# An attention and two-MoE-layer kernel in fp32 on one core: GpSimd's arithmetic given to VectorE and ScalarE, with shorter start-up groups and a new instruction list

## The chip, the cores and the metric

The kernel runs on one core of a Trainium2 chip. The metric is the device time of one execution in microseconds (us). Three runs of the kernel before took 591.71, 591.72 and 592.02 us; the median, 591.72, is the time before. A core has five engines that are spoken of here: TensorE (PE), VectorE (DVE), ScalarE (ACT), GpSimd (POOL) and SyncE (SP), which issues the transfers.

## What is computed

A sparse attention is followed by two feed-forward layers, all in float32 with inputs of 2 batches, 8 heads, 768 positions and head size 64, that is 1536 tokens of width 512.

```python
k_sum = k.reshape(B, H, nb, 32, D).max(axis=3)
v_sum = v.reshape(B, H, nb, 32, D).mean(axis=3)
scores_l = scale * q @ k.T                     # kept where |i - j| < 16
scores_s = scale * q @ k_sum.T + log(32)
a = softmax(concat([scores_l, scores_s]))
x = a @ concat([v, v_sum])
...
xn = x / sqrt(mean(x * x) + 1e-6) * rms_g
x = (silu(xn @ w_gate) * (xn @ w_val)) @ w_out     # d_ff 1536
...
h = x @ w_in
out = where(h > 0, h, exp(min(h, 0)) - 1) @ w_out2   # d_ff 2048
```

## The kernel before

**Attention.** Each batch is worked off in 6 pairs of 64-position tiles, so there are 12 pairs. For a tile the program builds `ka` (`copy_keys`: 96 neighbouring keys and the 24 block maxima `ksum`), the scores of a pair's two head halves come out of PE (`scores`, L462), DVE adds the mask and takes the row maximum (`add_mask` L467, `row_max` L471; the first four pairs get their mask from PE in `premask`), ACT does the exponentials and their sums (`exps`, L478), `guard` (L484) adds 1e-9 to the sums, `invert` (L488) takes reciprocals, `normalize` (L493 to L498) multiplies, PE transposes (`turn_e`, L503, tile `at`), a copy makes `ats`, PE applies the values `va` (`apply_v2`, L515, tile `pv`), and a copy puts the result into `xT`. The block means of `v` are placed into one of four `va` tiles (`place_v`) and repeated into the others (`repeat_v`, L375).

**Feed-forward.** The 1536 tokens are three blocks of 512. fp32 products are made of three fp32r products of high and low parts, so each operand is split: a cast makes the high part (L135, on ACT) and a subtraction the low part (L146, tiles `ws` for weights, `act..l` for activations). Weights come as 64-bit floats (`st`) and are turned into fp32 (`raw`) in `convert_a`, `convert_l`, `convert_b` (L259 to L279): DVE does that in two passes (L270, L279), or ACT and DVE in one each (L267, L275). Block 0 goes through both layers by itself, one chunk of 128 hidden columns at a time (`pg`, `pv_..c`, tanh gate `th` in L727 to L738, then `acc`; in the second layer `ph`, `ex`, `acc`), beside the attention of the later tokens. Blocks 1 and 2 are then done jointly with seven half-size products in place of eight (`add_joint`, L937 and L1116, tiles `w_1u`, `wd`, `td`). Norms go through sums of squares (`square`, `add_square` L589), a power on POOL (`root`, L607) and a diagonal product on PE.

**What sets the order.** Every operation is added with the engines it may run on, a cost and a due time (`add`, a dictionary of engines and costs where there is a choice), but the order of issue is a list of numbers written into the file, `PLAN`: each number divided by 4 names the operation, the remainder which of its engines takes it. `TAGS` says which of the PSUM banks or buffers a tile gets where it has a choice. The list was made ahead from the costs. Each engine executes its instructions in the list's order, so an instruction that waits holds up all behind it on that engine.

**POOL's part before.** Besides masks, selectors, zeros and the roots, POOL has 6 normalisations, 2 copies of keys, 4 repeats of `va`, 2 additions of squares, 24 low parts of weights (8 `ws_g`, 5 `ws_v`, 4 `ws_o`, 2 `ws_i`, 5 `ws_p`) and 5 of activations. The choices come from these lines:

```python
ANY_2 = {DVE: 0.6}, {POOL: 1.28, DVE: 0.6}, {POOL: 1.28}
...
LO_0, LO_1 = (1, 1, 1), 0
```

`LO_0` picks the entry of `ANY_2` for the weights of block 0.

**The start.** While the first keys are on their way PE multiplies zeros (`keep_warm`, L1227, tile `warm`) in groups, each `WARM_LONG.get(i, 2)` products long; a group in `AFTER_K` first multiplies a piece of a loaded key tile, so it can't begin ahead of that load. Group 1, behind the tile kT_0, has eight.

## Time and profile before

| | |
|---|---|
| median of three runs | 591.72 us |
| profiled execution: own time | 592.67 us |
| profiled execution: span from the first to the last instruction | 591.0 us |
| busy: PE, DVE, ACT, POOL | 574.1, 547.3, 430.4, 69.6 us |
| mean TensorE clock granted | 1.00 of full speed |
| bytes moved by transfers | 108.79 MB, 184 GB/s |

All rows quoted below are of that one profiled execution, whose own time is 0.95 us over the median. Busy times are unions of instructions' spans; instructions of one engine overlap a little in the trace, so the spacing from start to start is the price of one in a row. "Idle before" names the instruction that ended the engine's wait. A chain of waits is followed back from the last instruction of the stretch asked for, at each step to what released it.

### The profile page before, as it was taken

How to read it: one execution, taken by the hardware profiler on the slowest of the kernel's cores; microseconds unless marked ns; L12 is line 12 of the kernel's file. 1: busy time of each engine (PE TensorE's matmuls, PEld its weight loads, DVE VectorE, ACT ScalarE, POOL GpSimd, SP SyncE). 2: the span in 40 equal slices, each digit the busy share in tenths (PEclk: the TensorE clock that was granted, in tenths of full speed). 3: DMA queues.
4: the chain of work that ended last, by engine and by line, in shares of the span. 5: the costliest groups of instructions: out<-in, count | busy, mean ns of one | idle time of the engine just before them, and what ended most of it. 6: DMA issues, size and time to landing. Idle time of an engine off the chain costs nothing.

```text
span 591.0 us, 9948 instructions
## 1 busy us (share of the span) xinstructions
PE 574.1 (97%) x3366; PEld 467.6 (79%) x3366; DVE 547.3 (93%) x1049; ACT 430.4 (73%) x953; POOL 69.6 (12%) x89
## 2 busy tenths in 40 slices
PE   7799989999999999999999999999999999999997
PEld 3588768788877888888888888888888888888886
DVE  5999999999989988989998999999999999999993
ACT  3889978998988988646534456676666989788750
POOL 3326425024100031100000000000000000000000
PEclk9999999999999999999999999999999999999999
DMA  8888889988978977142134416324316552742202
GB/s 318 287 297 280 303 303 321 325 300 282 312 231 273 318 232 265 55 159 71 55 91 161 143 50 188 92 81 142 107 38 196 200 159 78 244 129 65 71 35 107
DMA packets 56051, 108.79 MB, mean 184 GB/s; under 512 B 6784, under 2 KB 19584, under 8 KB 56000
## 3 DMA queue, kind: packets, MB, share of 16 engines
q1 hardware_dynamic: 56000, 108.16, 56.2%
q8 instruction: 26, 0.43, 0.3%
q14 instruction: 25, 0.20, 0.1%
HBM read 79.82 MB, written 28.31 MB: 183 GB/s over the span
## 4 chain that ended last, share of the span: by engine, by line
PE 81%; DVE 9%; ACT 6%; issue 2%; DMA 1%; POOL 0%; DVEq 0%; ACTq 0%; POOLq 0%
PE acc L766 11%; PE B_1u L937 8%; PE ph L710 7%; PE C_1u L937 6%; PE A_1u L937 6%; PE B_2d L1116 6%; PE B_2u L937 6%; PE B_1d L1116 4%; PE C_2d L1116 4%; PE A_2d L1116 4%; PE C_2u L937 4%; PE A_2u L937 4%; PE C_1d L1116 3%; PE A_1d L1116 3%; PE pg L710 2%
## 5 line engine op out<-in xcount | busy, mean ns | idle before, releaser
L710 PE MATMUL ph<-xa,ws_i 128*128 128x512 f32 x192 | 48.0, 395 | 0.6 <-DVE ex L747 0.6
L937 PE MATMUL B_1u<-xh,w_1u 128*128 128x512 f32 x144 | 47.8, 391 | 0.0
L710 PEld LDWEIGHTS ph<-xa,ws_i 128*128 128x128 f32 x192 | 35.5, 188 | 8.8 <-DVE ex L747 1.0
L710 PE MATMUL pg<-xs,ws_g 128*128 128x512 f32 (+1 forms) x168 | 36.4, 364 | 0.7 <-DVE th L734 0.7
L1116 PE MATMUL B_2d<-td,wd 128*128 128x512 f32 x144 | 34.6, 389 | 0.0
L146 DVE TENSOR_TENSOR wd<-rd,wd 128x512 fp32r<-128x512 f32 x49 | 32.8, 684 | 0.2 <-ACT wd L135 0.2
L937 PE MATMUL C_1u<-xh,w_1u 128*128 128x512 f32 x96 | 32.8, 390 | 0.0
L710 PEld LDWEIGHTS pg<-xs,ws_g 128*128 128x128 f32 x168 | 28.1, 189 | 5.5 <-DVE th L734 0.9
L937 PE MATMUL A_1u<-xh,w_1u 128*128 128x512 f32 x96 | 32.3, 390 | 0.0
L135 ACT CAST wd<-rd 128x512 fp32r<-128x512 f32 x49 | 29.1, 621 | 4.1 <-PE B_2u L937 2.2
L937 PEld LDWEIGHTS B_1u<-xh,w_1u 128*128 128x128 f32 x144 | 27.0, 188 | 6.1 <-ACT h_1u L135 0.3
L937 PE MATMUL B_2u<-xh,w_2u 128*128 128x512 f32 x96 | 31.6, 389 | 0.0
L1116 PEld LDWEIGHTS B_2d<-td,wd 128*128 128x128 f32 x144 | 27.0, 188 | 5.6
L937 PE MATMUL B_1u<-xl,w_1u 128*128 128x512 f32 x72 | 28.1, 390 | 0.0
L1116 PE MATMUL B_1d<-td,wd 128*128 128x512 f32 x108 | 26.5, 389 | 0.0
L478 ACT ACTIVATE e<-e,nm 128x120 f32<-128x120 f32 x64 | 24.5, 387 | 1.7 <-DVE nm L471 1.6
L135 ACT CAST td<-z 128x512 fp32r<-128x512 f32 x28 | 17.1, 619 | 11.7 <-DVE z L1098 11.6
L1116 PE MATMUL C_2d<-td,wd 128*128 128x512 f32 (+1 forms) x102 | 24.5, 377 | 0.0
L1116 PE MATMUL A_2d<-td,wd 128*128 128x512 f32 x96 | 24.0, 389 | 0.0
L1116 PEld LDWEIGHTS B_1d<-td,wd 128*128 128x128 f32 x108 | 20.3, 188 | 4.2
L135 ACT COPY h_1u<-B_1u 128x512 f32<-128x512 f32 x21 | 12.3, 587 | 12.9 <-PE B_1u L937 12.9
L937 PE MATMUL C_2u<-xh,w_2u 128*128 128x512 f32 x64 | 21.5, 389 | 0.0
(547 smaller groups left out, 1777.2 us busy)
## 6 DMA issues: line engine op xcount, KB each, us to landing
st_i<-in_moe_w_in SPq DMA_DIRECT2D x16, 512.0 KB, 4.4
st_p<-in_moe_w_out SPq DMA_DIRECT2D x16, 512.0 KB, 4.9
st_v<-in_moe_w_val SPq DMA_DIRECT2D x12, 512.0 KB, 6.8
st_g<-in_moe_w_gate SPq DMA_DIRECT2D x12, 512.0 KB, 6.1
st_o<-in_moe_w_out SPq DMA_DIRECT2D x12, 512.0 KB, 5.7
kept_i<-raw_i SPq DMA_DIRECT2D x16, 256.0 KB, 4.3
kept_p<-raw_p SPq DMA_DIRECT2D x16, 256.0 KB, 4.4
va<-in_v SPq DMA_DIRECT2D x20, 192.0 KB, 5.8
```

What stands on the lines that cost most here:

```text
L135: nc.scalar.copy(out=out, in_=in_)
L146: (nc.gpsimd if eng == POOL else nc.vector).tensor_sub(out, a, b)
L478: nc.scalar.activation(out=e[:, pr, :], in_=s[:, pr, :], func=AF.Exp, bias=nm[:, pr:pr + 1], accum_out=ss[:, pr:pr + 1])
L710: nc.tensor.matmul(pt[:, i], wt[:, a, kk * P:(kk + 1) * P], xt[:, c, i], start=(kk == 0 and n == 0), stop=(kk == KM - 1 and n == 2))
L766: nc.tensor.matmul(acc, wt[:, a, cs], ot[e], start=(first and n == 0), stop=(last and n == 2))
L937: nc.tensor.matmul(pt, wt[:, a, cs], xt[e][:, kk], start=first and kk == n == 0, stop=kk == 1 and n == 2, skip_group_check=not first)
L1116: nc.tensor.matmul(pt[:, h], wt[:, a, cs], xt[:, e, h], start=first and n == 0, stop=last and n == 2 and h.stop == TB, skip_group_check=i ...
```

## The change

From the fifth pair on, `copy_keys` and `normalize` have no choice of POOL any more. The low parts of weights and activations, the additions of squares and the repeats of `va` never have it. `guard` may now run on POOL, and 11 of the 24 do. The costs of `place_v` and of the zero products are changed in the tables. Zero products come in groups of two, three more groups stand behind key loads. `PLAN` and `TAGS` are new throughout, so that the order on every engine is another; PE's operations are the same ones otherwise, and so are SP's transfers.

```diff
--- before.py
+++ after.py
@@ -393,9 +393,9 @@
                 add(PE, 0.25, due + 0.5 + 0.1 * t, mean_own, t, r=[f"va{t}#a", "sel"], w=[vp])
 
     def add_place(b, due, gap):
-        add({ACT: 0.72, DVE: 0.6} if b == 0 else {ACT: 0.8, DVE: 0.85}, 0, due, place_v, b, r=[f"vm{b}" if b else f"vp{b}"], w=["va0#s"])
+        add({ACT: 1.2, DVE: 1.15} if b == 0 else {ACT: 1.15, DVE: 0.85}, 0, due, place_v, b, r=[f"vm{b}" if b else f"vp{b}"], w=["va0#s"])
         for i in range(1, VA):
-            add({POOL: 0.6, ACT: 0.52} if b == 0 else {POOL: 0.6}, 0, due + gap * i, repeat_v, i, r=["va0#s"], w=[f"va{i}#s"])
+            add({DVE: 0.34, ACT: 0.52}, 0, due + gap * i, repeat_v, i, r=["va0#s"], w=[f"va{i}#s"])
 
     def window(t):
         lo, hi = max(0, QT * t - W0), min(S, QT * t + QT + W0)
@@ -479,9 +479,9 @@
                 out=e[:, pr, :], in_=s[:, pr, :], func=AF.Exp, bias=nm[:, pr:pr + 1],
                 accum_out=ss[:, pr:pr + 1])
 
-    def guard(b, t):
+    def guard(eng, b, t):
         ss = T[f"ss{b}_{t}"]
-        nc.vector.tensor_scalar_add(ss, ss, 1e-9)
+        (nc.gpsimd if eng == POOL else nc.vector).tensor_scalar_add(ss, ss, 1e-9)
 
     def invert(b, t):
         ss = T[f"ss{b}_{t}"]
@@ -539,7 +539,7 @@
             if b * NQ + t >= MT:
                 add_window(b, t, due - 3)
             near = [f"kT{b}_{x}" for x in range(lo // (2 * P), (hi - 1) // (2 * P) + 1)]
-            add({POOL: 0.86, DVE: 0.45, ACT: 0.65}, 0, due, copy_keys, b, t,
+            add({POOL: 0.86, DVE: 0.45, ACT: 0.65} if early else {DVE: 0.45, ACT: 0.65}, 0, due, copy_keys, b, t,
                 r=near + far, w=[f"ka{b}_{t}"], new=[("ka", f"ka{b}_{t}")])
         ns = [f"{b}_{j}_{h}" for h in range(2)]
         kas = [f"ka{b}_{2 * j + n}" for n in range(2)]
@@ -559,9 +559,9 @@
             add(DVE, 0.56, at + 1.9, row_max, b, f"{j}_{h}", src, r=[src], w=[f"nm{n}"], new=[("nm", f"nm{n}")])
             add(ACT, 1.43 if pre else 1.5, at + 2.6, exps, b, f"{j}_{h}", pre, r=[f"nm{n}"] + [f"s{n}", f"pm{n}"] * pre,
                 w=[f"e{n}", f"ss{n}"], new=[("ss", f"ss{n}")])
-            add(DVE, 0.13, at + 4, guard, b, f"{j}_{h}", w=[f"ss{n}"])
+            add({DVE: 0.13, POOL: 0.25}, 0, at + 4, guard, b, f"{j}_{h}", w=[f"ss{n}"])
             add(DVE, 0.1, at + 4, invert, b, f"{j}_{h}", r=[f"ss{n}"], w=[f"rs{n}"], new=[("rs", f"rs{n}")])
-            add({POOL: 0.94, DVE: 0.58, ACT: 1.14}, 0, at + 4.3, normalize,
+            add({POOL: 0.94, DVE: 0.58, ACT: 1.14} if early else {DVE: 0.58, ACT: 1.14}, 0, at + 4.3, normalize,
                 b, f"{j}_{h}", r=[f"rs{n}"], w=[f"e{n}"])
             add(PE, 0.48, at + 5.2, turn_e, b, f"{j}_{h}", tags, r=[f"e{n}"], w=[f"at{n}"], new=[(tags, f"at{n}")])
             add(ANY, 0, at + 5.7, copy_e, b, f"{j}_{h}", r=[f"at{n}"], w=[f"ats{n}"],
@@ -584,9 +584,9 @@
         else:
             nc.vector.tensor_mul(t, x, x)
 
-    def add_square(eng, blk, cs, i):
+    def add_square(blk, cs, i):
         s = T[f"sq{blk}_{SQ[blk][0]}{i}"]
-        (nc.gpsimd if eng == POOL else nc.vector).tensor_add(s, s, T[f"sq{blk}_{cs}{i}"])
+        nc.vector.tensor_add(s, s, T[f"sq{blk}_{cs}{i}"])
 
     def sum_square(blk, i, w, n_sums, tag):
         pss = new(tag, f"pss{blk}{i}", [P, 4, 4])
@@ -659,7 +659,7 @@
             add({ACT: 0.52, DVE: 0.6}, 0, due + 0.5 * n, square, blk, cs, i, r=[f"{x}#t{t}" for t in range(lo // QT, hi // QT)],
                 w=[sq], new=[("t2", sq)])
             if n >= n_sums:
-                add({POOL: 1.28, DVE: 0.6}, 0, due + 0.6 * n, add_square, blk, cs, i, r=[sq], w=[first])
+                add(DVE, 0.6, due + 0.6 * n, add_square, blk, cs, i, r=[sq], w=[first])
         y = f"{blk}{i}"
         add(PE, 0.95 * f * n_sums * TB / w, due + 3, sum_square, blk, i, w, n_sums, tag,
             r=[f"sq{blk}_{cs}{i}" for cs in SQ[blk][:n_sums]], w=["pss" + y], new=[(tag, "pss" + y)])
@@ -755,7 +755,7 @@
     def add_act(src, dst, due, tag="act"):
         h, l = dst + "h", dst + "l"
         add(ANY_SB, 0, due, act_a, src, dst, tag, r=[src], w=[h], new=[(tag, h)])
-        add(ANY_2[1], 0, due + 0.6, act_b, src, dst, tag, r=[src, h], w=[l], new=[(tag, l)])
+        add(ANY_2[0], 0, due + 0.6, act_b, src, dst, tag, r=[src, h], w=[l], new=[(tag, l)])
 
     def down(names, ms, act, ws, first, last):
         ot, wt = (T[act + "h"], T[act + "l"]), T[ws]
@@ -1223,7 +1223,7 @@
         pt = new(BANKS, f"warm{i}", [P, 4, P])
         if i in AFTER_K:
             nc.tensor.matmul(pt[:, 0, :16], ones, T[f"kT0_{AFTER_K[i]}"][:, 0, :16], start=True, stop=True)
-        for _ in range(WARM_LONG.get(i, 2)):
+        for _ in range(2):
             nc.tensor.matmul(pt, idle_w, idle_w.unsqueeze(1).to_broadcast([P, 4, P]), start=True, stop=True)
 
     add("-", 0.0, 0, take, "act", "rk0", [P, TB], w=["rk0"], new=[("act", "rk0")])
@@ -1231,7 +1231,7 @@
         add("-", 0.0, 0, take, "vq", f"va{i}", [P, H, D], w=[f"va{i}"], new=[("vq", f"va{i}")])
     add_k(0, K0, 0.7)
     for i, at in enumerate(WARM_AT):
-        add(PE, 0.44, at, keep_warm, i, r=[f"kT0_{AFTER_K[i]}"] if i in AFTER_K else [], new=[(BANKS, f"warm{i}")])
+        add(PE, 0.55 if i in AFTER_K else 0.43, at, keep_warm, i, r=[f"kT0_{AFTER_K[i]}"] if i in AFTER_K else [], new=[(BANKS, f"warm{i}")])
     add_vsum(0, VS0, VS0 + MEAN, BANKS)
     add_place(0, VS0 + MEAN + 1.5, 0.3)
     add("SP", 0.5, 7.0, load_g, w=["g_sb"])
@@ -1272,170 +1272,170 @@
 K0, QL, VA, PM = 5.4, (1.9, 6.5, 9.0, 12.5), 4, 3
 
 PLAN = (
...
 )
 TAGS = (
...
 )
 SUMS = 1
 X_0 = 23.0, 30.0
-WARM_AT = (3.4, 3.9, 4.0, 7.5, 8.5, 9.5, 10.5, 13.0)
-AFTER_K, WARM_LONG = {1: 0, 2: 2}, {1: 8}
+WARM_AT = (3.4, 3.9, 4.0, 7.5, 8.5, 9.5, 10.5, 13.0, 7.8, 8.0, 8.2)
+AFTER_K = {1: 0, 2: 2, 8: 0, 9: 1, 10: 1}
 ACT_B = 0
-LO_0, LO_1 = (1, 1, 1), 0
+LO_0, LO_1 = (0, 0, 0), 0
 LEN_A, LEN_2, LEN_U, LEN_P = 9.3, 6.3, 9.7, 1.37
 
 
```

The list shows its effect in the built programs' order. The first place is POOL, about the middle of block 0's first layer. Before (`ws` are low parts of weights, `e` the exponentials being normalised, `va` the value tiles):

```order
L493 TENSOR_TENSOR e_4_0_646<-e_4_0_646,rs_4_0_990 128x480
L146 TENSOR_TENSOR ws_v_998<-raw_v_944,ws_v_998 128x512
L493 TENSOR_TENSOR e_4_1_647<-e_4_1_647,rs_4_1_984 128x480
L146 TENSOR_TENSOR ws_g_993<-raw_g_899,ws_g_993 128x512
L410 MEMSET va_187 32x512
L146 TENSOR_TENSOR ws_g_995<-raw_g_935,ws_g_995 128x512
L146 TENSOR_TENSOR ws_v_1107<-raw_v_1058,ws_v_1107 128x512
```

and of the change, at the same pair of tiles (`ss` are the sums that the guard is added to, `y0` a root):

```order
L484 TENSOR_SCALAR ss_4_0_812<-ss_4_0_812 128x4
L607 TENSOR_TENSOR y0slice(0, 256, None)_904<-ms0slice(0, 256, None)_891,mhalf 128x2
L410 MEMSET va_178 32x512
L607 TENSOR_TENSOR y0slice(256, 512, None)_928<-ms0slice(256, 512, None)_921,mhalf 128x2
L484 TENSOR_SCALAR ss_4_1_909<-ss_4_1_909 128x4
L408 MEMSET va_171 32x512
```

The two normalisations and the four subtractions have left POOL; two guards have come. The second place is DVE, around the first low part of an output weight, `ws_o`. Before:

```order
L738 SCALAR_TENSOR_TENSOR th_1_1033<-th_1_1033,pv_1c 128x512
L275 SCALAR_TENSOR_TENSOR raw_v_1221<-st_v_1169 128x512
L146 TENSOR_TENSOR ws_o_1002<-raw_o_431,ws_o_1002 128x512
L495 TENSOR_TENSOR e_5_1_755<-e_5_1_755,rs_5_1_1224 128x480
L738 SCALAR_TENSOR_TENSOR th_3_1175<-th_3_1175,pv_3c 128x512
```

and of the change:

```order
L146 TENSOR_TENSOR ws_g_1111<-raw_g_1030,ws_g_1111 128x512
L734 SCALAR_TENSOR_TENSOR th_3_1186<-th_3_1186,pg_3_1079 128x512
L146 TENSOR_TENSOR ws_o_1058<-raw_o_440,ws_o_1058 128x512
L275 SCALAR_TENSOR_TENSOR raw_g_1195<-st_g_1128 128x512
L488 RECIPROCAL rs_5_1_1223<-ss_5_1_1147 128x4
L734 SCALAR_TENSOR_TENSOR th_1_1122<-th_1_1122,pg_1_846 128x512
L146 TENSOR_TENSOR ws_v_1125<-raw_v_1051,ws_v_1125 128x512
L146 TENSOR_TENSOR act_0_0l<-th_0_1061,act_0_0h 128x512
```

Three subtractions that stood on POOL (`ws_g`, `ws_v`, `act_0_0l`) stand between DVE's gate operations now. The third place is PE at the start, ahead of the scores of pair 0 (`s_0_0`, L462; L446 is its premask). Before, the last of the eight products of the group behind kT_0 and what follows:

```order
L1227 MATMUL warm_229<-idle_w 128x512
L446 LDWEIGHTS ident_b
L446 MATMUL s_0_0_239<-mask_b_163,ident_b 128x480
L449 LDWEIGHTS ident_b
L449 MATMUL s_0_0_239<-log_lo,ident_b 128x4x24
```

and of the change:

```order
L449 MATMUL s_0_1_252<-log_lo,ident_b 128x4x24
L1225 MATMUL warm_256<-kT_0_205,ones 128x16
L1227 LDWEIGHTS idle_w
L1227 MATMUL warm_256<-idle_w 128x512
L1227 LDWEIGHTS idle_w
L1227 MATMUL warm_256<-idle_w 128x512
L462 MATMUL s_0_0_241<-ka_0_267,q_0_207 64x120
```

Both premasks stand ahead of that group now, the group has two products, and the scores follow it at once.

## Rows read from the trace of the kernel before

**Rows 1.** The page of the whole span: busy time and share of each engine

```profile
span 591.0 us, 9948 instructions
...
PE 574.1 (97%) x3366; PEld 467.6 (79%) x3366; DVE 547.3 (93%) x1049; ACT 430.4 (73%) x953; POOL 69.6 (12%) x89
```

**Rows 2.** Busy time by engine in stretches; columns as its head says

```profile
core 0: us, PE busy (x) PEld busy (x) DVE busy (x) ACT busy (x) POOL busy (x), PEclk, DMA share, GB/s
22.00:80.00 58.00, 50.59 (x575) 42.67 (x575) 56.91 (x115) 49.74 (x141) 24.84 (x26) 1.00 0.86 291
80.00:110.00 30.00, 29.68 (x215) 23.61 (x215) 27.23 (x53) 28.27 (x80) 8.98 (x10) 1.00 0.91 307
110.00:260.00 150.00, 148.94 (x926) 121.01 (x923) 135.50 (x260) 125.12 (x281) 28.39 (x21) 1.00 0.78 256
...
340.00:580.00 240.00, 240.00 (x1063) 198.57 (x1062) 238.43 (x433) 173.62 (x329) 0.00 (x0) 1.00 0.37 116
```

**Rows 3.** The chain of waits by line, asked for 22:80 and for 80:110

```profile
by line: issue 12.7%; ACT e L478 6.8%; DVE xs L690 6.7%; DVE raw_g L275 5.4%; DVE raw_g L279 5.1%; DVE e L467 4.9%; DVE th L727 4.5%; DVE ksum L323 4.3%; DVE nm L471 4.2%; DVE ss L484 3.5%; DVE ws_v L146 3.1%; DVE ws_o L146 3.1%; DVE raw_g 
...
by line: ACT e L478 14.9%; ACT st_o L259 11.7%; issue 9.5%; ACT st_o L267 9.4%; ACT e L498 7.6%; ACT st_v L259 5.7%; ACT ws_v L135 5.4%; ACT ws_o L135 5.1%; ACT va L135 4.0%; ACT ws_g L135 3.7%; DVE e L495 3.5%; ACT th L730 3.5%; ACT ats L1
```

**Rows 4.** Timeline, 66 to 78: start, duration, instruction, idle before it

```profile
68.49 3.00 POOL L146 TENSOR_TENSOR ws_g<-raw_g,ws_g 128x512 fp32r<-128x512 f32 x2
...
70.27 1.77 DVE L146 TENSOR_TENSOR ws_o<-raw_o,ws_o 128x512 fp32r<-128x512 f32 x1
...
72.09 0.73 PE L766 MATMUL acc<-act_0h,ws_o 128*128 128x512 f32 x2 [1.14 <-DVE ws_o L146]
...
77.10 1.26 ACT L498 ACTIVATE e<-e,rs 128x120 f32<-128x120 f32 x4 [3.47 <-DVE rs L488]
```

**Rows 5.** Timeline of DVE at 3, 177 and 257 us

```profile
2.86 0.60 DVE L195 CAST mask_b<-mask 128x96 bf16<-128x96 f32 x1 [1.15 <-POOL mask L170]
...
176.92 1.30 DVE L137 COPY ka<-ksum 128x96 f32<-128x96 f32 x1
...
257.90 1.78 DVE L856 TENSOR_TENSOR y_t<-xT,xT 128x512 f32<-128x512 f32 x1
```

**Rows 6.** Groups of DVE (busy us, mean ns, idle before); timeline at 577

```profile
L146 DVE TENSOR_TENSOR wd<-rd,wd 128x512 fp32r<-128x512 f32 x49 | 32.8, 684 | 0.2 <-ACT wd L135 0.2
...
L279 DVE SCALAR_TENSOR_TENSOR raw_g<-st_g,raw_g 128x512 uint16<-128x512 uint16 x5 | 5.3, 1052 | 0.0
L279 DVE SCALAR_TENSOR_TENSOR raw_p<-st_p,raw_p 128x512 uint16<-128x512 uint16 x7 | 5.2, 753 | 0.0
...
576.91 1.29 DVE L146 TENSOR_TENSOR wd<-rd,wd 128x512 fp32r<-128x512 f32 x2
...
578.12 1.28 DVE L1106 TENSOR_TENSOR td<-z,td 128x512 fp32r<-128x512 f32 x2
```

**Rows 7.** Groups of POOL and, last, of DVE up to 262 us

```profile
L146 POOL TENSOR_TENSOR ws_g<-raw_g,ws_g 128x512 fp32r<-128x512 f32 x8 | 10.8, 1360 | 3.5 <-ACT ws_g L135 3.4
...
L137 DVE COPY va<-vp 24x128 f32<-24x128 f32 x4 | 1.2, 289 | 0.1
```

**Rows 8.** L484 by its line (min/median/max ns), then POOL's timeline

```profile
L484 DVE TENSOR_SCALAR ss<-ss x24: 144/170/1271, 14.7 to 212.1; 128x4 f32<-128x4 f32 x24
...
39.31 0.72 POOL L607 TENSOR_TENSOR 0slice(0, 256, None)_835<-0slice(0, 256, None)_820,mhalf 128x2 f32<-128x2 f32 x1 [0.82 <-DVE 0slice(0, 256, None)_820 L601]
```

**Rows 9.** Timeline of the start, 7 to 16 us

```profile
8.16 3.00 PE L1227 MATMUL warm<-idle_w 128*128 128x512 bf16 x8
...
9.35 0.20 DVE L143 TENSOR_SCALAR ka<-ksum 128x96 f32<-128x96 f32 x1
...
11.38 1.05 PE L462 MATMUL s<-ka,q 64*64 64x120 f32 x32
...
15.74 0.60 PE L1227 MATMUL warm<-idle_w 128*128 128x512 bf16 x2
```

**Rows 10.** Timeline of PE at the end

```profile
585.26 2.20 PE L1116 MATMUL A_2d<-td,wd 128*128 128x512 f32 x9
```

More of the change, by code (lines that the diff above doesn't have):

```diff
@@ L1274 @@
 PLAN = (
[151 rows of a table removed]
[151 rows of a table added]
 )
 TAGS = (
-    "5431670427554360163402637014263701703011001010011010100010101011001111010110100110101011010100110101"
-    "0100110110111202111122030251200046070134100202103225102171002142073026102530400711020076203251304120"
-    "0210200274121131530212712021120023160220475012011000202625221020003227246522021111002742110122203507"
-    "0022221200322001"
+    "2010303227655137432176032472012350137101200111010101010101010101100100101110010010110011001010101010"
+    "1011100111101100101201030050010206010017216401321221040111220240576202121010560111042500371111605012"
+    "2240320131241270025306072100210213122640172000115222002600010530111047231562102072202130141020070031"
+    "2412003101000321022"
 )
```

302 rows, old and new, of the table PLAN are left out of this document.

## The prediction, written before the changed kernel was run

> **What bounds the kernel now.** The page comes first [rows 1]: a span of 591.0 us with TensorE (PE) busy 97% and VectorE (DVE) 93%, ScalarE (ACT) 73%, GpSimd (POOL) 12%. Two engines are nearly full, so a share of busy time decides nothing and I go by stages. In the table of stretches [rows 2] DVE is idle for only 1.1 of the 58 us from 22 to 80; from 80 to 110 ACT is the fullest after PE (1.7 us idle); from 110 to 260 and on, PE is full, and from 340 to 580 both PE and DVE are (DVE idle 1.6 of 240). The chain of waits, asked for the same stretches [rows 3], agrees: until 80 us its largest shares are nearly all DVE's, from 80 to 110 ACT's (after 110 it is PE's but for single pieces). PE's work can't shrink: the new list holds the same matmuls (22 zero products before and after, three short ones more). So a gain has to come ahead of 260 us, where PE still waits, and DVE must not fall behind afterwards.
>
> The second thing to see is what POOL does to DVE [rows 4]. While POOL subtracts two weight pieces (68.49, 3.00 us), DVE's ws_o takes 1.77 us (70.27), and PE then sits 1.14 us idle for it. DVE alone takes 684 ns for such a subtraction [rows 6]. Over the whole trace 22 DVE instructions are over 0.1 us longer than usual for their kind, and all 22 overlap a POOL instruction: the first is the cast at 2.86 (0.60), the last the y_t at 257.90 (1.78) [rows 5]. Group means show it too: five raw_g of L279 average 1052 ns where raw_p of that line has 753 [rows 6]. Summed over the 22 the excess is 14.9 us: 6.8 in the eight from 22 to 80, 2.0 from 80 to 115, 5.3 from there on, 0.9 before.
>
> **The change, part by part.**
> *Off POOL.* 24 low halves of weights, 5 of activations and 2 square sums leave it (31 instructions; ws_g averages 1360 ns on POOL [rows 7]) for DVE, where such instructions follow each other every 0.60 us (two in 576.91 to 578.12 [rows 6]): +18.6 us of DVE. Five repeats of va go to DVE; no row has that copy on DVE, bounds are 0.29 (its copy of a quarter, [rows 7]) and 0.68 (a full tile): I take 0.42 for SBUF to SBUF, +2.1. Two weight conversions more by the two-pass way: +0.8.
> *Off DVE.* Eleven guards of 0.17 [rows 8]: -1.9. Four ats, four xT, two bank seeds, two squares go to ACT: 12 x 0.60, -7.2; two root copies, three pieces of keys, one normalisation and one xs: -2.6. So DVE's own work rises by 18.6 + 2.1 + 0.8 - 11.7 = +9.8 us. Against it stand the 14.9 us of overlap. They don't all go, since the early normalisations, one copy of keys, the roots and the guards stay on POOL. Bounds for what remains: 0.9 (what the overlaps before 22 us cost now) and 5 (eleven guards of up to 0.3 more); I take 2, nearer to the row. Net on DVE: 9.8 - 14.9 + 2 = -3.1 us.
> *On ACT.* The 12 copies and squares at 0.50 to 0.57 (+6.3), copies of keys (+2.4), roots, one normalisation and an xs (+2.4), less casts, joins and va (-2): about +9 us over the run. ACT's idle time covers it after 110 us (25 of 150 idle [rows 2]); ahead of 110 ACT's list up to the eighth tanh, summed in the same way as DVE's below, is 2.6 us longer.
> *Guards on POOL.* A guard sits between ACT's exponentials and DVE's reciprocal, so behind it waits DVE's whole queue. Its price on POOL is bounded by its own 0.17 on DVE and a 128x2 power's 0.72 on POOL [rows 8]; the list puts other DVE work between, so I cost it at nothing; without that cover it is at most eleven times 0.55 or 6 us, in places where PE mostly has work. The Trainium skill (SBUF — State Buffer, "SBUF: two separate sides") says that a GpSimd instruction and a DVE one with two SBUF inputs take a shared port pair as an exclusive lock, the later one waiting for the whole of the earlier. By that rule a guard could also wait out a whole DVE instruction and 31 moved ones could have cost up to 31 x 1.3 = 40 us; the trace has 14.9.
> *The start.* Scores of pair 0 begin at 11.38 though their keys are there at 9.55 (9.35 + 0.20 on DVE): PE is inside the group of eight zero products (8.16, 3.00 us) and then does a premask [rows 9]. With groups of two, one group stands between the keys' load and those scores. Bounds: -1.8 (all of the wait), and +1 if PE stays slow for longer: a pair of zero products takes 0.60 at 15.74, and four pairs took 3.00 at 8.16, so early ones are slower by some 0.2 to 0.4 a pair, and three short groups could pay it. I take -1. The key loads change order (kT_1 ahead of kT_0): all three are needed for the block maxima, so nothing.
>
> *The sum.* 22 to 80 us, DVE: twelve of the 31 fall here (+7.2), three va (+1.3); seven guards, two root copies, one xT, one xs and three e pieces less, and conversions put off. With each kind at its usual spacing in this trace, the new list holds 1.7 us less DVE work than the old one up to the fifth gate product of L727, and 6.4 us more up to the fifth L738; minus the 6.8 of overlap, plus 1 that stays, that is -7.5 and +0.6, on average -3.5. In 80 to 110 ACT takes over as the limit: +2.6, but of its idle time 3.47 us were one wait for DVE's reciprocal at 77.10 [rows 4], which should shrink. I keep -2.5 of the two stretches. After 110 only 1.1 us of overlap stands on the chain (ka at 176.92 [rows 5], 1.30): -0.5 after ACT's extra work. Start -1.0, middle -2.5, block 2 -0.5: **-4.0 us**. The tail allows it: DVE's last split ends at 579.4, 8.1 us ahead of PE's end at 587.5 [rows 10], and DVE's sum falls by 3.1. The profiled execution took 592.67 us, 0.95 more than the median 591.72, so I forecast 588.7 on its scale and **587.7** on the median's.
>
> **Rivals.**
> *DVE takes back what it is given (no change).* Stretch by stretch the 18.6 us of moved work can eat the overlap: up to the fifth L738 it is already +0.6. For it: DVE is full in two stretches and ACT's relief comes late; against: the whole-run sum is -3.1. Time: 591.5, within 0.2% of before, about what a measurement can tell from no change. The Trainium skill (Perfetto Trace Analysis, "Optimizing Scalar/DVE Operations") says that with DVE saturated, offloading to ScalarE or even GpSimd may make sense, which speaks against this change; it adds that the shared port may spoil it. By its first half alone DVE would pay +9.8 us; the overlap rows take more than that back.
> *ACT becomes the bound (slower).* Place: 80 to 155 us. Its list is 2.6 us longer at the eighth tanh and 7.6 at the twelfth. It decides if the 3.47 us wait isn't recovered and if tanh and act casts come after the extra copies of ats and xT: then +2.6 by 110, and some 2.5 more where PE waits for activations, less 2 from the start and DVE: +3, 594.7. For it: ACT is busy 28.27 of 30 us there. Against: much of the 7.6 is work of the later products done early (the first pair split of the joint stage stands 18 us of DVE work earlier in the new list), which can wait in nobody's way.
> *All of it arrives (faster still).* The 6.8 of overlap go and ACT keeps up: -1.8 - 6.8 + 1 - 0.5 = -8, 583.7. Against: ACT is the next limit from 80 us.
>
> **Chances.** Forecast 0.46, all of it 0.13, no change 0.14, ACT 0.27. From these: faster by over 0.2% 0.60 (0.46 x 0.95, 0.13, 0.03 of the no-change case), within 0.2% 0.12, slower 0.28. Lowest sum of the bounds: -1.8 - 6.8 - 1.1 = -9.7 or 582; highest: +1, +2.6 with 1 left of overlap, +1 later: 597. Leaving 2 in 10 outside, mostly above, the range is 582.5 to 594.5; the forecast's own is 585 to 590.
>
> **What would show it.** Right: DVE groups lose their long ones (raw_g of L279 near 755 ns), POOL's busy time falls from 70 to about 25 us, first scores begin near 10 us, and the first up product of the joint stage starts some 4 us earlier, with PE full from there on. Wrong: DVE reciprocals that wait for POOL, pairs of zero products still far over 0.60 us behind 11 us, a chain from 80 to 150 that is ACT's throughout, or PE gaps behind 340 us with DVE full, which would mean that DVE had fallen behind.

## The result, and the profile after

The changed kernel takes 584.85 us (median of four runs, 584.01 to 585.87), beside 591.87 us for the kernel before. The ratio is 0.9876, 95% interval [0.9852, 0.9900], so the kernel is faster by 7.0 us where I had forecast 4.0. It lies inside the range, between the forecast of 587.7 and the rival "all of it arrives" (583.7), and nearer to that rival, and just under the 585 to 590 that the prediction gives as the forecast's own range. The profiled execution took 585.12 us.

The page of the changed kernel, to be read against [rows 1]:

```profile
span 583.4 us, 9961 instructions
...
PE 573.9 (98%) x3372; PEld 468.4 (80%) x3372; DVE 544.0 (93%) x1058; ACT 437.1 (75%) x975; POOL 21.4 (4%) x61
```

PE's busy time is what it was, so the whole gain is idle time of PE: 591.0 - 574.1 = 16.9 us before, 583.4 - 573.9 = 9.5 now. DVE's busy time fell by 3.3 us (forecast: 3.1), POOL's to 21.4 (forecast: about 25), ACT's rose by 6.7 (forecast: about 9). The same stretches as in [rows 2]:

```profile
core 0: us, PE busy (x) PEld busy (x) DVE busy (x) ACT busy (x) POOL busy (x), PEclk, DMA share, GB/s
22.00:80.00 58.00, 56.61 (x607) 48.31 (x603) 57.47 (x125) 56.05 (x159) 7.99 (x14) 1.00 0.94 315
80.00:110.00 30.00, 30.00 (x249) 24.22 (x248) 29.08 (x59) 29.18 (x71) 0.81 (x2) 1.00 0.97 313
110.00:260.00 150.00, 149.93 (x894) 121.53 (x894) 139.80 (x276) 126.34 (x289) 3.25 (x6) 1.00 0.75 247
340.00:580.00 240.00, 239.89 (x1064) 198.35 (x1062) 231.36 (x417) 170.68 (x325) 0.00 (x0) 1.00 0.37 116
```

PE's idle time from 22 to 110 us fell from 7.73 to 1.39 us, from 110 to 260 from 1.06 to 0.07: 6.3 and 1.0 of the 7.4. What I had not expected is the column of ACT: from 22 to 80 it is busy 56.05 us where it was 49.74. The chain of waits of the changed kernel, for the stretches of [rows 3] (22 to 80 and 80 to 110), has become PE's own:

```profile
by line: PE pg L710 28.8%; PE acc L766 8.7%; PE pv L515 5.7%; PE pv_0c L710 5.5%; PE pv_3c L710 5.1%; PE pv_1c L710 5.0%; PE pv_4c L710 4.8%; PE pv_2c L710 4.7%; PE at L503 4.4%; DVE va L137 3.9%; ACT e L478 3.3%; PE vp L352 2.5%; ACT ats L
...
by line: PE acc L766 26.7%; PE pg L710 22.9%; PE pv L515 10.8%; PE pv_5c L710 10.0%; PE pv_7c L710 9.9%; PE pv_6c L710 9.8%; PE at L503 7.3%; PE s L462 3.3%; PE pv_8c L710 0.8%
```

The 22 long DVE instructions are gone without exception: no DVE instruction of the changed kernel is over 0.1 us longer than usual for its kind. The group that averaged 1052 ns in [rows 6] shows it; behind it stand the guards by their line (DVE and POOL, min/median/max ns):

```profile
L279 DVE SCALAR_TENSOR_TENSOR raw_g<-st_g,raw_g 128x512 uint16<-128x512 uint16 x5 | 3.7, 739 | 0.0
```

```profile
L484 DVE TENSOR_SCALAR ss<-ss x13: 135/164/170, 12.9 to 197.3; 128x4 f32<-128x4 f32 x13
L484 POOL TENSOR_SCALAR ss<-ss x11: 220/224/683, 18.3 to 174.2; 128x4 f32<-128x4 f32 x11
```

At the start (timeline of PE, then of DVE) the first scores begin 1.84 us sooner than in [rows 9]; then PE waits for a load of v, and DVE with it:

```profile
8.59 1.01 PE L1227 MATMUL warm<-idle_w 128*128 128x512 bf16 x2
9.54 1.11 PE L462 MATMUL s<-ka,q 64*64 64x120 f32 x32
...
20.92 1.19 PE L359 MATMUL vp<-va,own 96*32 96x128 f32 x24 [1.56 <-DMA va<-in_v]
...
22.18 1.20 DVE L137 COPY va<-vp 24x128 f32<-24x128 f32 x4 [1.72 <-PE vp L359]
```

### The profile page after: what moved, and what is told of

Its sections match the earlier page's. It is cut to its first block, busy times and chain, and to the rows that moved or that the text cites. A ratio compares the mean times of both kernels' runs of the same rounds, so it can differ in the third digit from the quotient of the medians.

```text
span 583.4 us, 9961 instructions
## 1 busy us (share of the span) xinstructions
PE 573.9 (98%) x3372; PEld 468.4 (80%) x3372; DVE 544.0 (93%) x1058; ACT 437.1 (75%) x975; POOL 21.4 (4%) x61
## 4 chain that ended last, share of the span: by engine, by line
PE 91%; DMA 4%; ACT 2%; DVE 1%; issue 0%; POOL 0%; SPq 0%; POOLq 0%; ACTq 0%
PE acc L766 12%; PE B_1u L937 8%; PE ph L710 7%; PE pg L710 6%; PE C_1u L937 6%; PE B_2d L1116 6%; PE B_2u L937 6%; PE A_1u L937 6%; PE B_1d L1116 4%; PE C_2d L1116 4%; PE A_2d L1116 4%; PE C_2u L937 4%; PE A_2u L937 4%; DMA va<-in_v 3%; PE C_1d L1116 3%; PE A_1d L1116 3%
## 5 line engine op out<-in xcount | busy, mean ns | idle before, releaser
L710 PE MATMUL ph<-xa,ws_i 128*128 128x512 f32 x192 | 46.8, 394 | 0.1
L146 DVE TENSOR_TENSOR wd<-rd,wd 128x512 fp32r<-128x512 f32 x49 | 32.6, 682 | 0.0
L135 ACT CAST td<-z 128x512 fp32r<-128x512 f32 x28 | 17.0, 619 | 11.5 <-DVE z L1098 8.0
```

Of the source, the lines that this page charges most:

```text
L135: nc.scalar.copy(out=out, in_=in_)
L146: (nc.gpsimd if eng == POOL else nc.vector).tensor_sub(out, a, b)
L710: nc.tensor.matmul(pt[:, i], wt[:, a, kk * P:(kk + 1) * P], xt[:, c, i], start=(kk == 0 and n == 0), stop=(kk == KM - 1 and n == 2))
```

## Experiments

The ratios are to the kernel before, which ran beside each. Line numbers in rows of an experiment can differ by a few from those of the changed kernel. In the names, b stands for an edit of the kernel before, a for one of the changed kernel.

| run | median, us | ratio [95%] |
|---|---|---|
| the change | 584.85 | 0.9876 [0.9852, 0.9900] |
| b_off31 | 595.61 | 1.0064 [1.0049, 1.0080] |
| b_engines | 619.00 | 1.0458 [1.0439, 1.0477] |
| b_short | 591.08 | 0.9987 [0.9977, 0.9997] |
| a_twice | 596.64 | 1.0084 [1.0071, 1.0097] |
| a_on31 | 590.13 | 0.9971 [0.9955, 0.9987] |
| a_long | 585.15 | 0.9887 [0.9868, 0.9906] |
| a_back | 596.38 | 1.0083 [1.0061, 1.0104] |
| a_guard | 586.00 | 0.9897 [0.9878, 0.9915] |
| a_vfirst | 584.57 | 0.9875 [0.9851, 0.9899] |
| a_act5 | 587.07 | 0.9912 [0.9896, 0.9927] |
| a_dve5 | 587.54 | 0.9923 [0.9904, 0.9943] |
| a_vwarm | 584.38 | 0.9862 [0.9842, 0.9883] |

### Does POOL's work cost DVE time by itself? (a_twice, beside a_guard)

```diff
+    def twice(kind, a, b, *_):
+        hi = T[a][:, 0] if kind == "split_b" else T[b + "h"]
+        x = T[b if kind == "split_b" else a].bitcast(F32)
+        for n in range(2):
+            cs = slice(256 * n, 256 * n + 256)
+            nc.gpsimd.tensor_sub(spare, x[:, cs], hi[:, cs].bitcast(F32))
...
+            if fn.__name__ == "guard":
+                eng = "DVE"
...
+            if i in TWICE:
+                self.again(fn.__name__, *args)
```

> The changed kernel with POOL doing 29 of the subtractions once more, in two halves of 256 columns each into a spare tile that nobody reads, at their places in the list; all 24 guards are on DVE, so that nothing but roots waits for POOL. DVE's and ACT's own lists stay what they are (but for 11 guards of 0.17). My theory, that a POOL subtraction costs DVE time by itself: 22 overlaps cost 14.9 us before, so DVE instructions that overlap POOL are again over 0.1 us longer than usual, 10 to 20 us in sum, DVE busy 555 to 565, time 588 to 594. Rival, the overlap in the trace of before was DVE waiting for results and buffers and POOL costs nothing: DVE busy 546, time 584 to 586.

The kernel a_guard has the second piece of this diff alone and is the one to compare with.

> The changed kernel with all 24 guards on DVE. My theory: a guard's place is worth nothing either way, 584.4 to 585.4; eleven times 0.17 = 1.9 us more on DVE against eleven waits of 0.22 on POOL and two hand-overs. Rival, DVE is so full that its 1.9 us reach the end: 586 or more. Second rival, the hand-overs cost: 583 to 584.

With POOL's second subtractions the time is 596.64 us against 586.00. DVE, whose list is the same in both, is busy 15.2 us longer (first a_guard's page, then a_twice's):

```profile
PE 573.8 (98%) x3372; PEld 468.4 (80%) x3372; DVE 544.9 (93%) x1069; ACT 437.4 (75%) x975; POOL 18.1 (3%) x50
```

```profile
PE 577.7 (97%) x3372; PEld 467.5 (79%) x3372; DVE 560.1 (94%) x1069; ACT 437.9 (74%) x975; POOL 79.9 (13%) x108
```

In a_guard no DVE instruction is over 0.1 us longer than usual for its kind, in a_twice 35 are, 17.8 us in sum. One place of the timeline of a_twice:

```profile
63.64 1.26 DVE L500 TENSOR_SCALAR ss<-ss 128x4 f32<-128x4 f32 x1
...
64.15 1.53 POOL L160 TENSOR_TENSOR spare<-raw_g,ws_g 128x256 bf16<-128x256 f32 x2
```

A guard on four columns takes 1.26 us instead of 0.17; it begins ahead of POOL's two halves and ends, at 64.90, about when the first of them does. Nobody reads the results of those halves, so it is no wait for data: the theory holds, and the rival (POOL costs nothing) falls. DVE's busy time came out as expected (555 to 565), but the time is above my 588 to 594. A buffer that POOL still reads could hold up others as well; the trace has one such wait, of ACT, 1.06 us at 217.88.

a_guard itself is 1.15 us over the change. That misses my 584.4 to 585.4 and meets the number of its rival (586 or more), but the two intervals overlap, and in its profile a load of v landed 0.4 us later too. Whether the place of the guards is worth something stays open between nothing and some 3 us.

### Is giving DVE the work, by itself, the gain? (b_off31, a_on31, b_engines)

b_off31 and b_engines keep the old order. The first gives the 31 operations to DVE, the second gives every operation the engine that it has in the changed kernel:

```diff
+            if eng == "POOL" and fn.__name__ in ("split_b", "act_b", "add_square"):
+                eng = "DVE"
```

```diff
+            eng = next((e for e, ops in ELSEWHERE.items() if i in ops), eng)
...
+ELSEWHERE = {
+    "DVE": (
...
```

> The kernel before, its list untouched, with the 31 subtractions and additions of POOL (24 low halves of weights, 5 of activations, 2 additions of squares) on DVE at the same places of the list. My theory: the gain is a trade, in which DVE takes 31 x 0.60 = 18.6 us, gets back most of the 14.9 us of overlap (some 10, since normalisations and a copy of keys stay on POOL), and needs the copies that went to ACT to come out even. Without those: DVE busy near 547.3 + 18.6 - 10 = 556 us, the time 591 to 597, most likely 594. First rival, POOL's overlap is all that the change pays for, whatever DVE is given: 585 to 588. Second rival, the list is all: 592 within 1.

> The kernel before, its list's order untouched, with every operation on the engine that it has in the changed kernel (64 moved to DVE, 48 to ACT, 15 to POOL); the zero products as before. My theory, in which the engines matter more than the order: DVE busy near 544 us as in the changed kernel, overlap below 2 us, time 587 to 589 (586.4 for the engines' and lists' part of the gain with the start, -1.5, not taken). First rival, the order makes it: 591 or more, since the old order was made for other engines. Second rival, the engines make all of it and the start nothing: 585.

a_on31 keeps the new order and gives the 31 back to POOL:

```diff
+            if i in ON_POOL:
+                eng = "POOL"
```

> The changed kernel, its list untouched, with the same 31 subtractions and additions back on POOL at their places. My theory: DVE busy near 544 - 18.6 + 10 to 15 of overlap = 535 to 540, POOL busy near 60, but 31 low parts come 0.8 us or more later and DVE's reciprocals wait behind guards that stand in POOL's queue: time 588 to 594. First rival, the list alone makes the gain and POOL is as good a place: 584 to 586. Second rival, relieving DVE helps: below 584.

The page of b_off31, then that of a_on31 with a group of POOL:

```profile
PE 575.6 (97%) x3366; PEld 469.6 (79%) x3366; DVE 553.7 (93%) x1080; ACT 430.5 (73%) x953; POOL 23.5 (4%) x58
```

```profile
PE 575.7 (98%) x3372; PEld 469.9 (80%) x3372; DVE 546.1 (93%) x1027; ACT 437.6 (74%) x975; POOL 67.8 (12%) x92
```

```profile
L152 POOL TENSOR_TENSOR ws_g<-raw_g,ws_g 128x512 fp32r<-128x512 f32 x8 | 11.7, 1463 | 15.7 <-ACT ws_g L141 15.6
```

In b_off31 the long instructions shrink from 14.9 us to 2.7 while DVE takes 18.6 more: 547.3 + 18.6 - 12.2 = 553.7, which is the page's figure, and the kernel is 0.64% slower, inside my 591 to 597. "POOL's overlap is all" (585 to 588) falls. How much of the 3.8 us is DVE's added work is not shown, because in this run PE was also granted about half its clock in two spells, 28 to 32 and 82 to 86 us, while it was busy throughout (two stretches of b_off31, columns as in [rows 2]):

```profile
28.00:30.00 2.00, 2.00 (x28) 1.88 (x24) 1.88 (x9) 2.00 (x9) 0.00 (x0) 0.53 0.90 270
84.00:86.00 2.00, 2.00 (x6) 1.54 (x6) 2.00 (x6) 0.99 (x6) 1.37 (x4) 0.50 0.59 127
```

By my estimate from these stretches and their neighbours (2 us each at 0.53, 0.62, 0.68, 0.50 and 0.97) the missing clock comes to 3.4 us of PE's time. So it is a_on31, and not this run, that tells against "the list is all". In a_on31 DVE is rid of the same 18.6 us and gets 20.2 us of long instructions in their place, so that it is busy 2.1 us more than in the change, without 31 instructions of its own (I had expected 535 to 540, and it is 546.1). The time is 5.3 us above the change and inside my 588 to 594: with the new list, which was made for the 31 on DVE, their place is worth 5.3 of the 7.0 us. In its profile PE has half its clock once, at 40 to 42, but the executions with a mean clock of 1.000 (588.39, 589.51 and 591.57) lie among the rest. POOL relieved DVE of nothing.

b_engines went far outside my theory (587 to 589); it falls to the first rival, the order, which had said 591 or more. DVE is no busier than before on its page (547.3 us), but the order that fitted the old engines doesn't fit the new ones; the waits of PE between 22 and 260 us begin so:

```profile
PE pg L715 <- DVE th L739: 4.8, 2, 2.5
PE at L508 <- DVE e L500: 4.4, 3, 3.3
PE pg L715 <- DVE th L743: 3.9, 2, 2.3
```

DVE itself is idle for 39.9 of these 238 us (it is busy 198.07), because each engine works its list in order and stands behind an instruction that came too early. PE's clock over the same stretch averages 0.96, so part of the loss is lost clock. Of the two orders tried, the new places are worth something only with the new one.

### Was ACT's relief needed? (a_back)

```diff
+            if i in TO_DVE:
+                eng = "DVE"
+            elif i in TO_ACT:
+                eng = "ACT"
```

> The changed kernel with the copies of ats, xT, bank seeds, root copies and squares on the engines that they had before (18 go back to DVE, 4 to ACT), the list's order untouched. My theory, that ACT's relief is what lets DVE take POOL's work: DVE busy + 8, near 552, PE idle between 22 and 110 us up by 2 to 4, time 586.5 to 589. Rival, ACT was the engine that was short: 583 to 584.5. No change within 0.5 would say that both have room in these stretches.

It costs 11.5 us, far more than my 586.5 to 589 allowed and more than the 8.2 us that DVE's busy time rises by (to 552.2). Part of that is again order and not work: from 22 to 260 us DVE's waits are headed by three for PE.

```profile
DVE ats L142 <- PE at L508: 6.0, 3, 4.2
```

So the direction is that of my theory (the copies belong on ACT in this list), but the sum of work does not give the size. The list was made for copies on ACT, and a_back doesn't separate what ACT's relief is worth from what a list with other engines costs, as in b_engines.

### What was the start worth? (b_short, a_long)

```diff
-AFTER_K, WARM_LONG = {1: 0, 2: 2}, {1: 8}
+AFTER_K, WARM_LONG = {1: 0, 2: 2}, {}
```

> The kernel before with two zero products in place of eight in the group behind kT_0, nothing else. My theory: the first scores begin at 9.5 to 10 us instead of 11.38, and as PE and DVE wait for one another until 40 us, 1 to 1.8 us of it reach the end: 590.1 to 590.9. First rival, DVE and ACT are full from 22 us whatever the first scores do: 591.9. Second rival, PE is granted or runs slower for longer after so few zero products: scores above 1.05 us for 32, time above 592.2.

```diff
-        for _ in range(2):
+        for _ in range(8 if i == 1 else 2):
```

> The changed kernel with eight zero products in place of two in the first group behind kT_0. My theory: the first scores begin 1.2 to 1.8 us later, near 11 us, and 1 to 1.8 us of it reach the end: 585.9 to 586.7. Rival, the start is made up for by 40 us: 584.9. Second rival, the warmer PE pays for a part: below 584.6.

On the kernel before the short group is worth 0.13%, about 0.8 us, though the first scores begin at 9.21, 2.17 us sooner. Behind them PE stood at an old wait (3.03 us for a copy at 26.66), and it was granted half its clock for a while (stretches of b_short; PEclk is the last column but two):

```profile
24.00:26.00 2.00, 0.00 (x0) 0.00 (x0) 1.71 (x6) 0.56 (x3) 1.11 (x2) 0.97 0.89 287
26.00:28.00 2.00, 1.34 (x25) 1.37 (x27) 2.00 (x7) 2.00 (x13) 0.00 (x0) 0.50 0.86 230
28.00:30.00 2.00, 2.00 (x19) 1.88 (x17) 1.64 (x8) 1.62 (x5) 0.00 (x0) 0.50 0.70 199
```

On the changed kernel the long group costs nothing that can be measured (585.15 against 584.85, with some 1.8 us of uncertainty). What shows more is the trace. First scores at 11.19 instead of 9.54, and yet DVE's copies out of the value means start at 22.09, where the change has 22.18:

```profile
11.19 1.05 PE L462 MATMUL s<-ka,q 64*64 64x120 f32 x32
...
22.09 1.20 DVE L137 COPY va<-vp 24x128 f32<-24x128 f32 x4
```

What is won ahead of the scores is spent in the 1.56 us in which PE waits for a load of v. By this trace the rival (made up for by 40 us) holds, and my theory of 1 to 1.8 us doesn't.

### Is the load of v then the limit? (a_vfirst, a_vwarm)

In the list, the load of the first output weight goes behind the loads of v, and ACT's passes over it behind the third pair's exponentials (codes 1688, 1692 and 1697; `...` stands for the codes between):

```diff
-    ... 304, 308, 1688, 128, 228, 232, 1732, 1737, 236, 312, 160, 152, 316, 340, 168, 268, ... 440, 1692, 1697, 349, ...
+    ... 304, 308, 128, 228, 232, 1732, 1737, 236, 312, 160, 152, 316, 340, 168, 1688, 268, ... 440, 349, ... 476, 1692, 1697, ...
```

> The changed kernel with the 512 KB of the first output weight (st_o) loaded behind the four loads of v that the first value means need, and ACT's two passes over it moved behind the exponentials of the third pair; nothing else. After the run with eight zero products, where first scores 1.6 us later cost nothing, my theory is that at 22 us the loads of v hold the kernel, so that the earlier scores bought nothing: here the last of them lands 1 to 1.4 us sooner (near 20.4 instead of 21.64), DVE's copies out of the means begin near 21, and 0.5 to 1.3 us of it reach the end: 583.6 to 584.4. Rival, DVE and ACT are full from 22 to 40 us and set the time whatever the loads do: 584.8 to 585.2. Second rival, ACT or DVE then waits for st_o: above 585.5.

DVE's copies begin 1.1 us sooner, and the median doesn't move: six executions spread from 582.67 to 587.49. The two slowest (586.52 and 587.49) are those with a mean clock of 0.996; the four at 1.000 took 582.67 to 585.18. In the profiled one, at 0.996, PE was idle for 2.11 of the 8 us from 28 on and then got half its clock; the change is idle for 1.30 of the same 8 us and keeps 1.00 (stretches of a_vfirst):

```profile
28.00:36.00 8.00, 5.89 (x137) 4.67 (x135) 8.00 (x20) 8.00 (x25) 2.56 (x4) 1.00 0.91 306
...
38.00:40.00 2.00, 2.00 (x12) 2.00 (x11) 1.54 (x4) 2.00 (x8) 0.48 (x1) 0.50 1.01 395
```

The last run puts zero products into those gaps:

```diff
+            if i in (165, 191, 149):
+                self.zeros(i)
...
+    def zeros(i):
+        pt = new("a1", f"zero{i}", [P, 4, P])
+        for _ in range(2):
+            nc.tensor.matmul(pt, idle_w, idle_w.unsqueeze(1).to_broadcast([P, 4, P]), start=True, stop=True)
```

> The run with the loads of v first, and in addition three pairs of zero products on PE between 29 and 37 us (behind the scores of the fifth and sixth pair and behind the fourth pair's values), into a bank that nothing else uses then. In the run without them DVE's copies of the means began at 21.08 instead of 22.18 and the fifth pair's exponentials 0.9 us sooner, but PE was granted half its clock in 38 to 40 us, behind a stretch in which it was idle for 2.1 of 8 us, and executions with a mean clock of 0.996 took 586.5 and 587.5, those with 1.0 took 582.7 to 585.2. My theory: the earlier loads are worth 1 us where the clock holds, and the zero products hold it: 583.3 to 584.3, no execution above 586, granted clock 1.0 from 36 to 42 us. Rival, the loads gain nothing even at full clock: 584.5 to 585.5. Second rival, the added products stand in PE's way or the clock falls all the same: 585.5 or more.

The stretches of a_vwarm, then two places of its timeline:

```profile
28.00:36.00 8.00, 7.55 (x147) 5.42 (x145) 8.00 (x18) 8.00 (x25) 2.56 (x4) 1.00 0.88 300
...
38.00:40.00 2.00, 2.00 (x19) 2.00 (x19) 2.00 (x6) 2.00 (x5) 0.67 (x1) 1.00 0.91 303
```

```profile
20.66 1.20 DVE L139 COPY va<-vp 24x128 f32<-24x128 f32 x4
...
67.69 0.68 ACT L261 ACTIVATE st_g<-st_g 128x512 f32<-128x512 f32 x1 [0.91 <-DMA st_g<-in_moe_w_gate]
```

The clock holds and no execution is above 585.12. The fifth gate product of DVE (L727) starts 0.84 us ahead of the change's. ACT, however, has waited 0.91 us for a load of a gate weight by 67.69, a wait that the change doesn't have, and at the first up product the lead is 0.03. At 584.38 it can't be told from the change: what the earlier loads of v won is gone again after the wait for a later load. This is the lowest median of the study, but not a version shown to beat the change.

### Where is the limit between 80 and 110 us? (a_act5, a_dve5)

```diff
+    TWICE = ('ws0_v7', 'ws0_g7', 'ws0_o2', 'ws0_o4', 'ws0_o3')
...
-        copy(eng, t[:, 0, cs], T[raw].bitcast(F32)[:, cs])
+        for _ in range(2 if ws in TWICE else 1):
+            copy(eng, t[:, 0, cs], T[raw].bitcast(F32)[:, cs])
```

a_dve5 does the same with the subtraction of `split_b`, for ws0_v6, ws0_v5, ws0_g7, ws0_o4 and ws0_o2.

> The changed kernel with five of ACT's casts of weights between 84 and 96 us done twice, 5 x 0.52 = 2.6 us more on ACT in the stretch in which my prediction had ACT as the limit, with just this +2.6 as its price. If ACT is the limit there: 587 to 587.5, with PE idle in 80 to 120. My theory now, that ACT's and PE's lists both have slack against one another there (ACT is busy 29.2 of 30 us, but PE never waits): less than 1 us of it, 584.8 to 585.8.

> The changed kernel with five of DVE's subtractions of weights between 80 and 94 us done twice, 5 x 0.60 = 3.0 us more on DVE. If DVE is the limit there: 587.3 to 587.9. If PE, which never waits between 40 and 210 us, is: 584.8 to 585.8. My theory: DVE is nearer to its limit than ACT (the chain from 26 to 40 us is DVE's and ACT's, and 11 guards of 0.17 cost about 1 us), so more of the 3.0 comes through than of ACT's 2.6: 585.5 to 587.5.

Of ACT's 2.6 us 2.2 reach the end, of DVE's 3.0 us 2.7 (medians against the change, each with some 1.7 us of uncertainty). Two of a_dve5's six executions had a mean clock of 0.996 and took 588.92 and 588.98; the other four, at 0.999 to 1.000, lie between 586.09 and 587.63. My expectation of less than 1 us for ACT was wrong. The stretch from 80 to 110 of a_act5, with two waits of DVE from its timeline, and then the same of a_dve5, with a wait of ACT:

```profile
80.00:110.00 30.00, 28.28 (x234) 21.57 (x233) 26.91 (x53) 29.71 (x69) 0.15 (x1) 1.00 0.87 288
```

```profile
85.63 0.69 DVE L736 SCALAR_TENSOR_TENSOR th<-th,pg 128x512 f32<-128x512 f32 x1 [0.90 <-ACT th L732]
88.50 0.69 DVE L275 SCALAR_TENSOR_TENSOR raw_v<-st_v 128x512 uint32<-128x512 uint32 x1 [1.02 <-ACT st_v L267]
```

```profile
80.00:110.00 30.00, 28.22 (x234) 21.35 (x233) 29.70 (x59) 26.98 (x64) 0.36 (x1) 1.00 0.88 285
```

```profile
84.62 0.64 ACT L732 ACTIVATE th<-th 128x512 f32<-128x512 f32 x1 [0.86 <-DVE th L729]
```

The two runs mirror each other. With more on ACT, DVE waits for ACT and sinks to 26.91 us; with more on DVE, ACT waits and sinks to 26.98; in both PE loses 1.7 to 1.8 us that it didn't lose before. In the changed kernel ACT, DVE and PE are in balance there, and none has slack to take more.

## Why the prediction was right, and where its size was off

**What bounds it, and POOL's price.** Right. The gain is PE's idle time, nearly all of it ahead of 260 us, and PE is full from the first up product on. The overlap of [rows 5] is POOL's doing, as a_twice shows.

**Off POOL, off DVE.** The net was -3.1 us and is 544.0 - 547.3 = -3.3. The match is in part luck. I left 2 us of overlap and none was left, so DVE's own work rose by 14.9 - 3.3 = 11.6 us where I had added up 9.8: two errors of about 2 us cancel. ACT's rise was 6.7 where I had 9.

**The start, -1.0: not found in the changed kernel.** The scores came 1.84 us sooner, beyond my lowest bound of -1.8 even, but in a_long they come 1.65 us later and nothing of that is left at 22 us; on the kernel before, b_short gives 0.8 us. I had read what stood ahead of the scores and not what comes next: the trace of before has no wait for v there, since it came to that point later. A bound was misread too. By the rows that the prediction quotes, an early pair of zero products is slower by 3.00 / 4 - 0.60 = 0.15 us, not by 0.2 to 0.4.

**The middle, -2.5: the term that failed.** It is worth -6.3 us by PE's idle time. Two readings were too small. First, DVE: I had its list at -7.5 us up to the fifth gate product of L727 and +0.6 up to the fifth L738, and took an average of -3.5. In the traces these two instructions start 9.9 us (78.76 to 68.83) and 1.9 us (81.27 to 79.36) sooner, 2.4 and 2.5 more than I had (L727, before and now):

```profile
78.76 0.69 DVE L727 TENSOR_TENSOR th<-pg,rk 128x512 f32<-128x512 f32 x1
68.83 0.68 DVE L727 TENSOR_TENSOR th<-pg,rk 128x512 f32<-128x512 f32 x1
```

Second, and larger, ACT. I set its 2.6 us of additional list up to the eighth tanh against one wait of 3.47 us [rows 4]. Its busy time up to there did rise, by 1.7 us, but its idle time up to there fell from 19.4 to 10.2 us, and the tanh comes 7.6 us sooner (all up to its start, columns as in [rows 2]; before, then now):

```profile
0.00:109.92 109.92, 97.64 (x998) 76.32 (x1000) 99.17 (x211) 90.51 (x268) 41.24 (x68) 1.00 0.89 302
0.00:102.36 102.36, 96.48 (x977) 76.43 (x978) 94.33 (x212) 92.19 (x273) 18.14 (x55) 1.00 0.94 311
```

ACT was full from 80 to 110 [rows 2], but only after it had been idle for 8.26 of the 58 us before, 7.8 of them in waits for DVE (3.5 for the reciprocal of [rows 4], 1.6 for a row maximum, 2.7 for conversions and the gate). The two longest, before:

```profile
ACT e L498 <- DVE rs L488: 3.5, 1, 3.5
ACT e L478 <- DVE nm L471: 1.6, 1, 1.6
```

In the changed kernel ACT's waits from 22 to 80 us are these, and none is for DVE:

```profile
ACT e L478 <- POOL e L493: 0.9, 1, 0.9
ACT st_v L259 <- DMA st_v<-in_moe_w_val: 0.7, 1, 0.7
ACT xT L135 <- PE pv L515: 0.2, 1, 0.2
```

With DVE's part done sooner, ACT's work of 80 to 110 began sooner, and the added work went into the old waits. A held-up DVE brings such idle time back where the list for ACT stays the same: up to the eighth tanh ACT is idle for 11.5 us in a_guard and 16.1 in a_twice, and for 12.5 in a_on31 beside the change's 10.2 (a_guard, a_twice, a_on31):

```profile
0.00:103.66 103.66, 96.76 (x978) 76.47 (x979) 94.97 (x220) 92.16 (x273) 15.54 (x47) 1.00 0.92 310
0.00:108.89 108.89, 98.03 (x976) 75.93 (x977) 100.16 (x220) 92.78 (x273) 46.25 (x75) 1.00 0.89 297
0.00:105.16 105.16, 97.95 (x976) 77.68 (x977) 92.84 (x196) 92.70 (x273) 39.38 (x70) 0.98 0.92 303
```

But a_on31, with the 31 back on POOL, keeps most of the fall from 19.4. So the larger part of it came with the new order and the other moves, and how the -6.3 us divides between order and a freer DVE stays open. A stretch that is full says what limits it, not how much of the work in it could have been done earlier.

**Block 2, -0.5.** It was -1.0 between 110 and 260 us. The three terms make 0 - 6.3 - 1.0 = -7.3; the spans differ by 7.6.

**The rivals.** "DVE takes back what it is given" is what happens to DVE in b_off31 (busy 6.4 us longer), where the old order stays and ACT takes nothing. The rule that I set beside it (the Trainium skill, Perfetto Trace Analysis, "Optimizing Scalar/DVE Operations": with DVE saturated, offload to ScalarE or even GpSimd) is supported here for ScalarE by a_back, as far as that run goes, and fails for GpSimd by a_on31; the 20.2 us there agree with its own caveat on the shared port. "ACT becomes the bound" has support for its mechanism, since a_act5 passes most of 2.6 us on, but in the change itself the waits that went away paid for ACT's added work. "All of it arrives" gave -8 and came nearest; its -1.8 for the start didn't arrive, and its -6.8 + 1 for the middle was nearly the measured -6.3.

**The guards.** Costed at nothing; a_guard leaves that open and would allow up to some 3 us in favour of POOL. On POOL the longest of the eleven took 0.68 us, 0.46 over the usual 0.22, so none waited out a whole DVE subtraction (0.60).

**The signs.** raw_g at 739 ns (I had said near 755), POOL at 21.4 us, scores at 9.54 and zero products at 0.59 behind 11 us came as written. The first up product came 8.7 us sooner (256.11 to 247.43) instead of 4, of which 7.6 last to the end; none of the wrong signs appeared.

## What to carry to other kernels

Before an engine is called the next limit because one stretch shows it full, sum its idle time up to that point and what it waited for: if that was the engine being relieved, its waits may go too. Work given to GpSimd should be credited with what the trace shows it to take from VectorE, here as much as it gave. In a kernel whose engines work fixed lists, engines and order are one decision; moving the operations without the order cost 4.6%, and none of the halves tried gave the gain (a_on31, the new list with the 31 on POOL, came nearest, with 0.3% of the 1.2%).

## What the runs showed of the hardware

**Which DVE instructions POOL holds up.** Counted over the trace of before, for DVE instructions that overlapped POOL by at least half their usual length: those that read PSUM (L467, L734, L738), the row maxima of L471 and the reciprocals were never over 0.1 us long (0 of 32); subtractions of L146 were in 4 of 10, L275 in 4 of 11, and guards, one SBUF input of four columns, in 3 of 5, by up to 1.1 us. In a_twice L146's kind was long in 17 of 34. One PSUM reader is among the 35 there (a gate product at 63.71); it stands right behind the held guard and ends with it, at 64.90. The Trainium skill (SBUF — State Buffer, "SBUF: two separate sides") names DVE instructions with two SBUF inputs, or in a mode that uses both port pairs, as the ones that lock against GpSimd. The subtractions agree with the first half; the guards, with one input, are long too, and whether they run in such a mode no run here shows.

**The clock after a gap.** In b_short PE had no work from 24 to 26 us and had 0.50 of its clock (1.2 of 2.4 GHz) from 26 on; in a_vfirst it was idle 2.11 of 8 us in small gaps and had 0.50 at 38 to 40. In a_vfirst the executions that lost clock are the slowest, and in a_vwarm three pairs of zero products kept the clock at 1.00; that in b_short the lost clock took back part of the earlier start is likely but not shown.
